# Nyström attention followed by a SiLU feed-forward layer on one core: four second-layer products, one landmark tree and some vector work are moved to other slots

## The chip, the cores and the metric

The kernel runs on one core of a Trainium2 chip. The metric is the device time of one execution in microseconds (us). Before the change three runs took 259.84, 260.09 and 260.16 us, with a median of 260.09 us. The engines are named as in the profile: PE is the matmul engine and PEld its weight loads, DVE the vector engine, ACT the scalar engine, POOL the GpSimd engine, SP the queue from which output writes and DMA transposes are issued.

## The reference

For each of 8 batches and 8 heads (576 tokens, 64 dimensions a head) the reference computes a Nyström approximation of attention and puts its result through a two-layer network:

```python
q_lm = q.reshape(B, H, 32, 18, D).mean(axis=3)      # 32 landmarks a head
k_lm = k.reshape(B, H, 32, 18, D).mean(axis=3)
A  = softmax(q    @ k_lm.T / sqrt(D))               # 576 x 32
Bm = softmax(q_lm @ k_lm.T / sqrt(D))               # 32 x 32
C  = softmax(q_lm @ k.T    / sqrt(D))               # 32 x 576
Z  = Bm.T / (norm1(Bm) * norminf(Bm) + 1e-6)
for _ in range(6):
    Z = 2 * Z - Z @ Bm @ Z
x = A @ Z @ C @ v                                   # 8 heads side by side: 4608 tokens x 512
h = x @ w_in                                        # 512 -> 2048
out = (h * sigmoid(h)) @ w_out                      # 2048 -> 512
```

## The kernel before

The work is a pipeline over batches, with the order of every engine written out by hand. Each engine executes its instructions in program order, and an instruction waits for semaphores of the engines and transfers whose data it needs.

**Periods and slots.** Batch b has a period of 16 slots. In slot s, `l1(s)` multiplies two 128-column blocks of the folded first layer (`mb`, which is Z·C·v·w_in of that batch) with the transposed attention matrix `AT` into a PSUM tile `hps`, and `act(s)` has ACT apply SiLU from `hps` into `gT`. Slots 0 to 7 cover the first half of the batch's tokens and 8 to 15 the second. `hps` comes from a ring of two PSUM tiles (`ps2`, two banks each), which is also used by the tiles `scp`, `sa`, `mpp`, `ctp` and, in some places, `lmp`. So a matmul into such a tile waits until the tile before last has been read.

**The second layer** is a queue. `l2_mm(n)` issues the next n products `ops` (`gT` block times `w_out`, 512 columns). After 16 products a block of 128 tokens is complete; ACT copies it to `ost`, and SP writes it out. The table `CNT` says how many products each slot of batches 0, 1 and 2 issues; later batches use `REST`. The products are the filler that PE does between steps that wait for other engines.

**The attention of the next batch** is computed inside the same slots. Its steps, each named by its method: scores and softmax of B and C (`b_scores`, `c_scores`, `c_max`, `c_exp`, `b_norm`, `b_expand`), the iteration for Z on PE and DVE (`f_mm`, `b_scale`, `f_out`, then pairs `ns_mm` on PE and `ns_step` on DVE, the last with `x_out`), C·v (`w_scale` takes reciprocals of C's sums on DVE in four small operations; `w_mm`, `w_out`), its product with Z (`z_mm`, `z_out`), and the fold with `w_in` (`m_unit` or `m_pair`: PE products, then copies into `mb` by DVE and ACT). The matrix A is normalized by `a_norm(i)`: a sum and a reciprocal on DVE and a multiplication on POOL (`an`). For batches 0 and 1, PE transposes A (`a_transpose`, copied by `a_out` into `AT`); from batch 2 on, DVE does (`a_back`). From batch 2 on, C's exponentials go to `eCT` by DMA transposes issued from SP, and A's scores go through DVE transposes `xs`, maxima `nm`, a subtraction on POOL (`a_sub`) and one exponential on ACT (`a_exp_all`).

**Landmarks.** Sums over 18 tokens are made by PE (`landmarks_pe`, tile `lmp`) or, from batch 2 on, by a tree of five additions on POOL (`landmarks_pool(b, j)`: tiles `lma`, `lmb`, `lmc`, `lmd`, `lmn`), each tree for two of the four loaded arrays `nat` of a batch (j = 0 or 2). `lm_t` transposes the landmarks on DVE.

**Loads** are issued from POOL's queue (`load_qk`, `load_v`), so each stands in line with POOL's arithmetic.

Batch 0's period has the attention of batch 1 from slot d = 2 on; in the code `r = s - d`. Batch 1's period has the attention of batch 2 from slot d = 3 on. In slot d of batch 1, `a_pair` computes the scores `sa` of batch 2 and `a_sub` follows on POOL. In slot d + 3 = 6, `f_mm` to the first `ns_mm` stand around the products. In slot 15 of batch 1, `lm_t` and `a_pair` of batch 3 are issued. The lines that matter before the change: `m_unit` at 735 to 756, `CNT` at 847, the landmark sum in slot 1 of batch 1 at 988 to 991, `rest` and `m_unit(2, ...)` at 1051 to 1061, the steps r = 5 to 8 at 1097 to 1120, and the trees at 1207.

Of the kernel before, what the change touches and what calls it, by code (L numbers as in the profile page):

```python
# [43 lines left out]
def kernel(  # L44
# [9 lines left out]
    nc = tc.nc  # L54
# [28 lines left out]
    def ps2(nm):  # L83
        return psh.tile([128, 2, 512], FP, tag="h", name=nm)
# [16 lines left out]
    def load_qk(b, js=(1, 0, 3, 2)):  # L101
        if b not in nat_t:
            nat_t[b] = loadp.tile([128, 4, SEG * Dh], BF, tag="nat", name="nat")
        nat = nat_t[b]
        for j in js:
            src = (q, k)[j % 2]
            g = j // 2
            nc.gpsimd.dma_start(
                out=nat[:, j, :],
                in_=src[b, 4 * g:4 * g + 4].rearrange("h (l t) d -> (h l) (t d)", t=SEG))  # L110
# [136 lines left out]
    class Att:  # L247
# [484 lines left out]
            copy(out=self.AT[:, :, self.ar[0]:self.ar[1]], in_=self.at)  # L732


        def m_unit(self, f, *copy, parts=1, between=None, pair=False, before=None):
            self.m_done = f + 1
            if f == 0:
                mb_t[self.b] = attp.tile([128, 2, DFF], BF, tag="mb", name="mb")
            if pair:
                m2 = ps2("mpp")  # L740
                m = [m2[:, 0, :], m2[:, 1, :]]
            else:
                m = [psa1("mp"), pso1("mp")]
            for j in range(4):
                for r in range(2):
                    p = slice(64 * r, 64 * r + 64)
                    mm(m[r][32 * j:32 * j + 32, :], self.zwT[p, j, :],
                       w_in_sb[p, j, 512 * f:512 * f + 512], start=True, stop=True)
            if before:
                before()  # L750
            for c0 in range(0, 512, 512 // parts):
                if c0 and between:
                    between()
                for r in range(2):
                    c = slice(c0, c0 + 512 // parts)
                    copy[1 if c0 else r](out=mb_t[self.b][:, r, 512 * f:512 * f + 512][:, c], in_=m[r][:, c])

# [80 lines left out]
    def l2_add(b, *blocks):  # L840
        for i in blocks:
# [2 lines left out]
            l2_state["queue"] += [(b, 128 * i, c, c + w) for c in range(0, DM, w)]  # L844


    CNT = {0: [0, 0, 0, 0, 4, 4, 2, 2, 4, 4, 3, 3, 2, 2, 1, 1],
           1: [1, 0, 1, 4, 2, 12, 12, 0] + [4] * 8,
           2: [8, 4, 12, 12, 3, 3, 2, 2, 3, 3, 3, 3, 3, 2, 2, 7]}
    REST = [3, 4, 12, 12, 3, 2, 2, 2, 4, 4, 4, 3, 3, 3, 3, 8]  # L850

# [20 lines left out]
    a = Att(0)  # L872
# [68 lines left out]
    for b in range(B):  # L941
# [3 lines left out]
        a0 = a  # L945
        a, ready = ready, None

        d = (2, 3)[b] if b < 2 else 0
# [5 lines left out]
        def act(s):  # L954
            l1_act(b, s, h.pop(s))

        for s in range(NDC):
# [3 lines left out]
            if s <= d and b == 0:  # L961
# [5 lines left out]
                elif s == 1:  # L967
                    a0.m_unit(1, nc.scalar.copy, nc.scalar.copy, parts=2,
                              between=lambda: act(1))
# [6 lines left out]
                if s == 0:  # L976
                    a = Att(1)
# [3 lines left out]
            elif not nxt or s <= d:  # L981
                l1(s)
                act(s)
                n = cnt[s]

                if s == 0 and b % 2:
                    l1_tail(b)
                if b == 1 and s == 1:
                    lp = ps2("lmp")[:, 0, :]
                    landmarks_pe(2, lp, 2, 2)  # L990
                    landmarks_out(2, lp, 2, 2)
# [44 lines left out]
            elif s == d + 2:  # L1036
# [11 lines left out]
                a.a_shift(0)  # L1048
                a.a_exp(0)

                def rest():
                    for i in (1, 2):
                        a.a_shift(i)
                        a.a_exp(i)
                    a.c_transpose(0)
                    a.b_expand()
                    l2_mm(2)
                    a.f_mm()
                    a.b_scale()

                a0.m_unit(2, nc.vector.tensor_copy, nc.scalar.copy, pair=True, before=rest)
                table(AF.Silu)
                a.f_out()
                a.c_out(0)
# [5 lines left out]
            elif b == 0:  # L1070
# [4 lines left out]
                if r == 3:  # L1075
                    load_qk(3, (1,))
                    act(s - 1)

                    def step():
                        a.ns_mm()  # L1080
                        a.ns_step()
                        l1(s)

                    a0.m_unit(3, nc.scalar.copy, nc.scalar.copy, before=step)
                    nc.vector.tensor_tensor(out=parity, in0=mask[:, 0:2, 0],
                                            in1=mask[:, 2:4, 0], op=OP.add)
                elif r == 4:
                    a.ns_mm()
                    a.ns_step()
                    act(s)  # L1090
                    a0.a_transpose(1)
                    a0.a_out(nc.vector.tensor_copy)
                    a.c_transpose(1)
                    a.c_out(1)
                    a.a_norm(0)
                    load_qk(3, (0,))
                elif r == 5:
                    act(s)
                    a.ns_mm()
                    a.ns_step()  # L1100
                    a.w_scale()
                    a.a_norm(1)
                elif r == 6:
                    a.ns_mm()
                    a.ns_step()
                    a.a_norm(2)
                    load_qk(3, (3,))
                elif r == 7:
                    a.ns_mm()
                    a.ns_step()  # L1110
                    load_qk(3, (2,))
                    landmarks_pool(2, 0)
                elif r == 8:
                    a.ns_mm(last=True)
                    a.x_out()
                    act(s)
                    l2_mm(n)
                    n = 0
                    a.a_transpose(0)
                    a.a_out(nc.vector.tensor_copy)  # L1120
                elif r == 9:
                    act(s)
                    transpose_qk(2, ORD[0])
                    l2_mm(n)
                    n = 0
                    a.w_mm()
                    a.w_out()
                elif r == 10:
                    a.z_mm()
                    a.z_out()  # L1130
                    transpose_qk(2, ORD[1])
                elif r == 12:
                    a.a_transpose(1)
                    a.a_out(nc.vector.tensor_copy)
                    transpose_qk(2, ORD[2])
# [60 lines left out]
            if b == 0:  # L1196
                if s == 3:
                    load_qk(2)
            elif b + 2 < B:

                if b == 1 and s == 9:
                    load_qk(4)
                if s == 14 and b + 4 < B:
                    load_qk(b + 4)
                if s == 7 + d // 2:
                    load_v(b + 2)
                if s in (4 + d, 8 + d):
                    landmarks_pool(b + 2, (s - 4 - d) // 2)

                if s == 13 and b > 1:  # L1210
                    ready = Att(b + 2)
                    ready.lm_t(0, 2)
                ts = (7, 8, 10, 12) if d == 0 else (8, 9, 10, 11)
                if s in ts:
                    transpose_qk(b + 2, ORD[ts.index(s)])
                if s == 15 and b == 1:
                    ready = Att(b + 2)
                    ready.lm_t(0, 2)
# [38 lines left out]
```

## Time and profile before

| | before |
|---|---|
| median of 3 runs | 260.09 us |
| the profiled execution's own time | 260.13 us |
| its span, first to last instruction | 258.4 us |
| PE busy | 243.5 us (94%) |
| ACT busy | 169.8 us (66%) |
| DVE busy | 163.4 us (63%) |
| POOL busy | 128.2 us (50%) |
| granted TensorE clock | 1.000 |

Rows of a timeline give the start in us from the span's start, the duration in us, the engine, the source line, the operation, what is written and read, and the shape; in brackets stands the engine's idle time before the instruction, and what ended it. Several similar instructions close together are merged into one row (x4), whose duration then goes from the first start to the last end. A row of the chain of waits gives start, share of the end's path in us, engine, tile and line. Matmuls overlap: the distance between two starts is shorter than one matmul's duration. Some matmul records are missing from the trace (554 of the products appear, against 592 loads of their weights), so a hole of about 0.22 us ahead of a product `ops` need not be a wait.

### The profile page before, as it was taken

What the parts mean: (1) busy time and instruction counts of PE and PEld (TensorE: products, weight loads), DVE (VectorE), ACT (ScalarE), POOL (GpSimd) and SP (SyncE); (2) the same over time, 40 slices, a digit from 0 to 9 for tenths busy, and PEclk for the clock granted to TensorE, in tenths of its full rate; (3) what the DMA queues carried; (4) which work ended last, traced back from release to release, by engine and by line L of the source; (5) the groups of instructions that cost most, each with busy time, mean ns of one, the idle gap of its engine ahead of it and who ended that gap; (6) DMA issues with size and microseconds to landing.
All of it is one profiled execution on the core that took longest, in us unless ns stands there. A gap on an engine that the chain in (4) does not pass through costs nothing.

```text
span 258.4 us, 6560 instructions
## 1 busy us (share of the span) xinstructions
PE 243.5 (94%) x2706; PEld 138.7 (54%) x2748; DVE 163.4 (63%) x375; ACT 169.8 (66%) x312; POOL 128.2 (50%) x156
## 2 busy tenths in 40 slices
PE   8979999989998999999999999999999999999994
PEld 2646555455554555556654564556545655556553
DVE  5878977858896859776885688667967545000000
ACT  2378975669746875778576957597669858445511
POOL 7716547713899379935993299319923030100000
PEclk9999999999999999999999999999999999999999
DMA  7999999971389993885289418122621500111122
GB/s 219 202 210 207 206 206 213 223 161 30 114 119 237 193 130 64 123 180 142 49 140 198 116 43 133 43 57 88 121 56 44 136 25 24 54 68 43 42 81 81
DMA packets 30061, 31.15 MB, mean 121 GB/s; under 512 B 10960, under 2 KB 21456, under 8 KB 30032
## 3 DMA queue, kind: packets, MB, share of 16 engines
q0 software_dynamic: 14816, 17.76, 42.0%
q1 hardware_dynamic: 15216, 12.98, 17.9%
q8 instruction: 21, 0.34, 0.5%
q14 instruction: 8, 0.07, 0.1%
HBM read 36.70 MB, written 9.44 MB: 179 GB/s over the span
## 4 chain that ended last, share of the span: by engine, by line
PE 73%; DVE 8%; POOL 7%; issue 4%; ACT 4%; DMA 3%; POOLq 0%; ACTq 0%
PE ops L80 39%; PE hps L80 20%; DMA eCT<-eC 3%; PE idle L80 3%; PE bb L80 2%; PE lmp L80 2%; POOL lma L232 2%; DVE cmx L449 2%; PE sa L80 2%; PE mp L80 2%; PE scp L80 1%; PE wp L80 1%; DVE nm L610 1%; PE mpp L80 1%; POOL xs L636 1%
## 5 line engine op out<-in xcount | busy, mean ns | idle before, releaser
L80 PE MATMUL ops<-w_out_sb,gT 128*128 128x512 bf16 (+1 forms) x554 | 138.6, 373 | 4.3 <-issue 3.6
L810 ACT ACTIVATE gT<-hps 128x576 bf16<-128x576 f32 (+2 forms) x128 | 82.6, 652 | 57.1 <-PE hps L80 54.9
L80 PE MATMUL hps<-AT,mb 128*128 128x288 bf16 (+2 forms) x512 | 83.0, 286 | 1.5 <-DVE xs L627 0.7
L80 PEld LDWEIGHTS <-gT 128*128 128x128 bf16 x592 | 54.2, 98 | 48.5 <-issue 8.8
L80 PEld LDWEIGHTS <-mb 128*128 128x128 bf16 x512 | 48.2, 98 | 27.4 <-issue 1.8
L203 DVE STREAM_TRANSPOSE qkT<-nat 128x576 f32<-128x576 f32 x32 | 39.1, 1243 | 0.2
L836 ACT COPY ost<-ops 128x512 f32<-128x512 f32 (+1 forms) x37 | 21.1, 572 | 14.6 <-PE ops L80 11.5
L232 POOL TENSOR_TENSOR lma<-nat 128x1152 f32<-128x1152 bf16 x11 | 26.2, 2381 | 0.4 <-DMA nat<-in_q_dram 0.3
L408 DVE SCALAR_TENSOR_TENSOR fx<-fx,bb 128x320 bf16<-128x320 bf16 (+1 forms) x39 | 17.9, 458 | 11.3 <-PE bb L80 10.5
L636 POOL TENSOR_TENSOR xs<-xs,nm 128x576 f32<-128x576 f32 x12 | 13.6, 1155 | 19.3 <-DVE nm L631 19.3
L776 DVE CAST mb<-mp 128x512 bf16<-128x512 f32 x28 | 18.0, 685 | 7.2 <-PE mp L80 7.2
L165 ACT ACT_TABLE_LOAD x16 | 20.5, 1283 | 1.1 <-PEq L1241 0.8
L1154 POOL COPY gate<-wsp 128x2 f32<-128x2 f32 x6 | 1.1, 186 | 30.7 <-DVE wsp L493 30.7
L692 POOL TENSOR_TENSOR an<-ex,arec 128x576 bf16<-128x576 bf16 x12 | 13.6, 1159 | 5.3 <-DVE arec L678 5.2
L80 PEld LDWEIGHTS <-fx 128*128 128x128 bf16 (+1 forms) x132 | 8.3, 94 | 12.2 <-DVE fx L408 5.2
L80 PE MATMUL bb<-fx 128*128 128x160 bf16 (+2 forms) x132 | 13.5, 212 | 1.2 <-DVE fx L408 1.1
L777 ACT CAST mb<-mpp 128x1024 bf16<-128x1024 f32 x14 | 14.2, 1012 | 0.0
L627 DVE STREAM_TRANSPOSE xs<-sa 128x576 f32<-128x576 f32 x12 | 8.7, 762 | 7.6 <-PE sa L80 7.6
L449 DVE TENSOR_REDUCE cmx<-scp 128x1 f32<-128x576 f32 x16 | 12.0, 752 | 0.5 <-PE scp L80 0.3
L663 DVE TENSOR_REDUCE arec<-ex 128x18 f32<-128x576 bf16 (+2 forms) x17 | 11.7, 689 | 0.0
L814 POOL COPY gT<-gT 128x1024 bf16<-128x1024 bf16 x4 | 4.1, 1037 | 14.9 <-ACT gT L810 14.9
L237 POOL TENSOR_TENSOR lmc<-lmb,lma 128x384 f32<-128x384 f32 x11 | 11.0, 1004 | 0.9
(120 smaller groups left out, 267.7 us busy)
## 6 DMA issues: line engine op xcount, KB each, us to landing
out_dram<-ost SPq DMA_DIRECT2D x35, 256.0 KB, 2.3
v<-in_v_dram POOLq DMA_DIRECT2D x8, 576.0 KB, 7.2
nat<-in_k_dram POOLq DMA_DIRECT2D x15, 288.0 KB, 7.8
nat<-in_q_dram POOLq DMA_DIRECT2D x15, 288.0 KB, 8.3
w_in_sb<-in_moe_w_in_dram POOLq DMA_DIRECT2D x4, 512.0 KB, 14.5
w_out_sb<-in_moe_w_out_dram POOLq DMA_DIRECT2D x4, 512.0 KB, 13.6
raw<-in_k_dram SPq DMA_DIRECT2D x1, 576.0 KB, 4.2
raw<-in_q_dram SPq DMA_DIRECT2D x1, 576.0 KB, 5.1
```

The costliest lines, as they stand in the source:

```text
L80: nc.tensor.matmul(out=o, lhsT=lhsT, rhs=rhs, start=start, stop=stop, skip_group_check=True)
L165: nc.scalar.activation(out=spare[:, 1:2], in_=spare[:, 0:1], func=func)
L203: nc.vector.transpose(out=o.rearrange("p (l t) -> p t l", t=SEG), in_=nat_t[b][:, j, :].bitcast(FP).rearrange("p (t l) -> p t l", l=L))
L232: nc.gpsimd.tensor_tensor(out=a1, in0=nat[:, :, 0:3 * w], in1=nat[:, :, 3 * w:6 * w], op=OP.add)
L408: nc.vector.scalar_tensor_tensor(out=n, in0=self.fx, scalar=2.0, in1=self.p, op0=OP.mult, op1=OP.add if self.tiled else OP.subtract)
L449: nc.vector.tensor_reduce(out=mx, in_=self.s[g][:, :, 0:HF], op=OP.max, axis=AX.XY, negate=True)
L636: nc.gpsimd.tensor_tensor(out=self.xs[:, i], in0=self.xs[:, i], in1=self.nm[:, i].unsqueeze(3).to_broadcast((128, 2, SEG // 2, L)), op=OP.add)
L692: nc.gpsimd.tensor_tensor(out=self.an[:, i].rearrange("p r t l -> p (r t) l"), in0=x, in1=r.unsqueeze(2).to_broadcast((128, SEG, L)), op=O ...
L776: nc.vector.tensor_copy(out=o[:, r, 0:512], in_=m[r])
L777: nc.scalar.copy(out=o[:, :, 512:1024], in_=m2)
L810: nc.scalar.activation(out=gT_t[b][:, 2 * s:2 * s + 2, o + c0:o + c1], in_=h[:, :, 0:c1 - c0], func=AF.Silu)
L836: nc.scalar.copy(out=ost[:, 0:hi - lo], in_=st["ps"][:, 0:hi - lo])
```

## The change

It has six parts.

1. `m_unit` gets a second callback. In slot 4 of batch 0 (r = 2), the shift and exponentials of A and the transposes of C stay ahead of the copies of `mb`; the expansion of B, two products, `f_mm` and `b_scale` come behind them. On PE nothing changes place; on DVE the copy into `mb` comes ahead of four small operations (`bdt`, `cs`, `n`, `nrm`) and no longer behind them.
2. The products of batch 0's slots 10 to 15 go from 3, 3, 2, 2, 1, 1 to 2, 2, 1, 1, 0, 2, four fewer. Those of batch 1's slots 0 to 6 go from 1, 0, 1, 4, 2, 12, 12 to 1, 1, 2, 7, 2, 12, 11, four more. The block of 16 that was finished in slot 15 of batch 0 is now finished in slot 2 of batch 1.
3. In slot 1 of batch 1 the product stands ahead of the landmark matmuls of batch 2.
4. `w_scale` of batch 1 moves from r = 5 to r = 8, behind `x_out`.
5. `a_norm(1)` of batch 1 moves from r = 5 to r = 6, and `a_norm(2)` from r = 6 to r = 7, each with its multiplication on POOL; the load of one array of batch 3 thereby comes ahead of the second multiplication.
6. Batch 3's tree for j = 0 moves from slot 7 to slot 0 of batch 1, and its tree for j = 2 from slot 11 to slot 7. On POOL the first now stands between the copy of `gT`'s tail and the subtractions of batch 2's `a_sub`; behind the second, the loads of batch 4 and those of batch 5 follow each other with no tree between.

```diff
-        def m_unit(self, f, *copy, parts=1, between=None, pair=False, before=None):
+        def m_unit(self, f, *copy, parts=1, between=None, pair=False, before=None,
+                   after=None):
...
+            if after:
+                after()
...
-    CNT = {0: [0, 0, 0, 0, 4, 4, 2, 2, 4, 4, 3, 3, 2, 2, 1, 1],
-           1: [1, 0, 1, 4, 2, 12, 12, 0] + [4] * 8,
+    CNT = {0: [0, 0, 0, 0, 4, 4, 2, 2, 4, 4, 2, 2, 1, 1, 0, 2],
+           1: [1, 1, 2, 7, 2, 12, 11, 0] + [4] * 8,
...
                 if b == 1 and s == 1:
+                    l2_mm(n)
+                    n = 0
                     lp = ps2("lmp")[:, 0, :]
...
-                def rest():
+                def first():
                     for i in (1, 2):
                         a.a_shift(i)
                         a.a_exp(i)
                     a.c_transpose(0)
+
+                def second():
                     a.b_expand()
                     l2_mm(2)
                     a.f_mm()
                     a.b_scale()
 
-                a0.m_unit(2, nc.vector.tensor_copy, nc.scalar.copy, pair=True, before=rest)
+                a0.m_unit(2, nc.vector.tensor_copy, nc.scalar.copy, pair=True, before=first,
+                          after=second)
...
                     a.ns_mm()
                     a.ns_step()
-                    a.w_scale()
-                    a.a_norm(1)
                 elif r == 6:
                     a.ns_mm()
                     a.ns_step()
-                    a.a_norm(2)
+                    a.a_norm(1)
                     load_qk(3, (3,))
                 elif r == 7:
                     a.ns_mm()
                     a.ns_step()
+                    a.a_norm(2)
                     load_qk(3, (2,))
                     landmarks_pool(2, 0)
                 elif r == 8:
                     a.ns_mm(last=True)
                     a.x_out()
+                    a.w_scale()
...
-                if s in (4 + d, 8 + d):
-                    landmarks_pool(b + 2, (s - 4 - d) // 2)
+                trees = (0, 7) if b == 1 else (4, 8)
+                if s in trees:
+                    landmarks_pool(b + 2, 2 * trees.index(s))
```

## The prediction

> **What bounds the kernel now.** I read the page first (spans, engines, chain), then the chain of waits over batches 0 and 1, then the timeline around every step that moves.
>
> ```profile
> PE 73%; DVE 8%; POOL 7%; issue 4%; ACT 4%; DMA 3%; POOLq 0%; ACTq 0%
> ```
>
> This is the chain that ended last: PE carries 73% of it, so what shortens the kernel is a wait of PE that goes away, or a product put where PE would have waited. After the wait at 96.43 us, quoted further down, the timeline shows none of PE's that is worth naming; whatever lead PE has there should reach the end. I therefore follow one number through the trace: by how much PE reaches each step earlier than before, the lead.
>
> **Slot 4 of batch 0: nothing.** Rows of the timeline:
>
> ```profile
> 32.30 0.59 ACT L756 CAST mb<-mpp 128x512 bf16<-128x512 f32 x1 [0.43 <-DVE mb L756]
> ```
> ```profile
> 35.00 1.62 POOL L697 TENSOR_TENSOR an<-ex,arec 128x512 bf16<-128x512 bf16 x2
> ```
> ```profile
> 36.67 0.44 PEld L725 LDWEIGHTS <-an 64*128 64x128 bf16 x4 [0.19 <-POOL an L697]
> ```
>
> ACT's copy waited 0.43 us for DVE's. With DVE's copy ahead of the four small operations, ACT's comes some 0.4 us earlier, and the first layer's matmuls behind it. But PE then transposes batch 0's second part of A, whose multiplication on POOL ends at 36.62; it hangs on a load issue and DVE sums that don't move. PE already waited for it. The lead there goes back to 0.
>
> **The sums and the scaling: 0.55 us.** DVE, then PE:
>
> ```profile
> 39.42 0.15 DVE L487 RECIPROCAL wsc<-csum 128x1 f32<-128x1 f32 x1
> 39.59 0.33 DVE L489 RECIPROCAL wsc<-csum 64x1 f32<-64x1 f32 x2
> 39.95 0.43 DVE L493 TENSOR_TENSOR wsp<-wsc,parity 128x4 f32<-128x4 f32 x1
> ```
> ```profile
> 41.18 0.43 DVE L408 SCALAR_TENSOR_TENSOR fx<-fx,bb 128x320 bf16<-128x320 bf16 x1
> ```
>
> ```profile
> 40.57 0.71 PE L80 MATMUL hps<-AT,mb 128*128 128x320 bf16 x4
> 41.66 0.31 PE L80 MATMUL bb<-fx 128*128 128x160 bf16 x2 [0.39 <-DVE fx L408]
> 41.81 1.03 PE L80 MATMUL ops<-w_out_sb,gT 128*128 128x512 bf16 x4
> 42.68 0.71 PE L80 MATMUL hps<-AT,mb 128*128 128x320 bf16 x4
> 43.22 0.20 PE L80 MATMUL bb<-fx 128*128 128x32 bf16 x2
> ```
>
> Two prices come from here: a product takes PE (42.68 - 41.81)/4 = 0.217 us, a slot's first layer 43.22 - 42.68 = 0.54. Without a wait, `bb` at 41.66 would start at 40.57 + 0.54 = 41.11. It waits because `ns_step` stands behind w_scale and a_norm(1) on DVE. After the change nothing stands between: lead 0.55. The a_norms fall into the next two slots, where DVE has room: the first took from `wsp`'s end at 40.38 to 41.18, 0.8 us, and a slot lasts 42.68 - 40.57 = 2.1. Their multiplications on POOL are needed only by the transposes of slots 10 and 14; that a load of batch 3 is now issued ahead of the second costs POOL's queue nothing that PE waits for.
>
> **Slot 10: DVE becomes the bound.** Here two products are taken out (0.43), but w_scale now stands in front of a_out:
>
> ```profile
> 43.46 0.45 DVE L424 SCALAR_TENSOR_TENSOR xb<-fx,bb 64x64 bf16<-64x64 bf16 x2 [0.96 <-PE bb L80]
> 44.45 0.56 DVE L732 COPY AT<-atp 128x768 bf16<-128x768 bf16 x1 [0.54 <-PE atp L725]
> ```
> ```profile
> 46.17 0.42 DVE L512 TENSOR_TENSOR wz<-wp,wsp 128x256 bf16<-128x256 f32 x1
> ```
>
> `xb` starts at 43.46 - 0.55 = 42.91 and ends at 43.36. w_scale takes 0.53 us up to `wsp`, and `wsp` itself 0.43 as above or less:
>
> ```profile
> 65.27 0.16 DVE L493 TENSOR_TENSOR wsp<-wsc,parity 128x4 f32<-128x4 f32 x1
> ```
> ```profile
> 39.32 1.04 POOL L697 TENSOR_TENSOR an<-ex,arec 128x512 bf16<-128x512 bf16 x1 [2.04 <-ACT gT L810]
> ```
>
> The long `wsp` ended at 40.38, just after POOL's multiplication (40.36); the short one, in batch 1, ran with POOL idle. Moved, `wsp` comes about 0.1 us behind POOL's last multiplication by my order, so I take 0.16. That puts the copy of `AT` at 43.36 + 0.69 = 44.05, or 0.1 sooner as neighbours on an engine overlap a little (the pair at 81.59 and 81.99 below: 0.05; for three pairs an estimate). `wz` follows the copy's start by 46.17 - 44.45 = 1.72, near 45.67: lead 0.5 for `wz` and the `z_mm` that waits for it. With 0.43 for `wsp` it is 0.25. PE itself would be nearly 1 us early; the two products buy nothing here.
>
> The Trainium skill ("SBUF — State Buffer", section "SBUF: two separate sides") says that a VectorE operation with two SBUF inputs and a GpSimd operation that reads SBUF exclude each other for a whole instruction. The pair of ends 40.36 and 40.38 agrees. By that rule any overlap would hold `wsp` to the end of POOL's instruction, and the kernel would come to about 258.55 and not 258.3.
>
> **Slots 12 to 15 and the start of batch 1.** Three products less and one more: 3 x 0.217 gives a lead of 1.15 before the last, of which I take off 0.1, an estimate between nothing and one product, because `hps` in slot 14 now comes close to ACT's previous `gT`. So 1.05 when ACT takes slot 15's `gT`, 0.83 when PE starts batch 1. There the chain of waits runs over ACT:
>
> ```profile
> 50.88 0.70 ACT gT L810
> 51.58 0.90 ACT mb L777
> 52.49 0.49 ACT ost L836
> 52.98 0.56 ACT gT L810
> 53.54 0.04 issue
> 53.58 1.17 PE lmp L80 x18
> ```
>
> The block's end moves to slot 2, so `ost` (0.49) leaves this chain, and `lmp` is released at 53.58 - 1.05 - 0.49 = 52.04. PE needs longer: its second first-layer group waits for the copy `mb` that ended at 51.58 + 0.90 = 52.48 and now ends at 51.43, then its four matmuls of 288 columns (0.54 x 288/320 = 0.49) and the added product: about 52.2. I take a lead of 1.3. Slot 2's added product lowers it to 1.1. `ost` now stands between two `gT` copies, with one slot's room. Its write goes out on SP some 2 us later, still ahead of batch 2's transposes; nothing else moves on that queue. Slot 3 gets three more products, in front of this wait:
>
> ```profile
> 57.88 0.28 PE L80 MATMUL hps<-AT,mb 128*128 128x288 bf16 x1 [0.66 <-DVE xs L627]
> ```
>
> They take 0.65; of the 0.66 idle, some is the pipeline's own, and I take 0.5. Lead behind them 0.95. `xs`, with its lead of 1.1, is then ready 0.15 before PE asks for it; that is the cover.
>
> **The tree in slot 0: must fit.** It stands on POOL behind the tail copy; `a_sub` and the gate copy queue behind it, and ACT's exponential waits for `a_sub`.
>
> ```profile
> L108 POOL DMA_DIRECT2D nat<-in_q_dram x1: 594/594/594, 40.3 to 40.3; - x1
> ```
> ```profile
> DMA to landing us min/median/max: 13.5/13.5/13.5
> ```
> ```profile
> 59.20 2.27 POOL L636 TENSOR_TENSOR xs<-xs,nm 128x576 f32<-128x576 f32 x2 [6.52 <-DVE nm L631]
> ```
> ```profile
> 62.91 1.15 ACT L643 ACTIVATE ex<-xs 128x1152 bf16<-128x1152 f32 x1
> ```
> ```profile
> 76.42 2.41 POOL L232 TENSOR_TENSOR lma<-nat 128x1152 f32<-128x1152 bf16 x1
> ```
> ```profile
> 81.59 0.45 POOL L240 TENSOR_TENSOR lmn<-lmd,lmc 128x128 bf16<-128x128 f32 x1
> 81.99 0.58 POOL L108 DMA_DIRECT2D nat<-in_k_dram  x1
> ```
>
> Its array of batch 3 was issued at 40.3 and landed at 53.8. A tree takes 82.04 - 76.42 = 5.62, so it ends near 59.45, although POOL was idle for 6.52 us before. `a_sub` (2.27) then runs 59.5 to 61.8; the exponential can start at 61.85, or 1.06 earlier than before. My lead is 0.95: the cover is 0.1 us, and beyond it every 0.1 of delay costs 0.1, because ACT's chain releases the next first layer in slot 7.
>
> Slot 6's removed product shortens the way to `ns_mm`; DVE's later `ns_step`s come earlier and with them a wait of PE's weight load:
>
> ```profile
> 72.43 0.11 PEld L80 LDWEIGHTS <-fx 128*128 128x128 bf16 x2 [0.51 <-DVE fx L408]
> ```
>
> Worth 0.2, one product: lead 1.15.
>
> **The tree that leaves slot 11: 0.4, and the transposes behind it: 0.25.**
>
> ```profile
> 82.45 0.32 PE L80 MATMUL sa<-qkT,lmc 32*32 32x288 bf16 x8 [0.36 <-DVE lmc L274]
> ```
> ```profile
> L466 SPq DMA_TRANSPOSE eCT<-eC x2: 1217/1254/1290, 88.3 to 89.7; - x2
> ```
> ```profile
> DMA to landing us min/median/max: 6.7/7.1/7.4
> ```
> ```profile
> 96.43 0.24 PEld L80 LDWEIGHTS <-eCT 96*32 96x32 bf16 x24 [0.25 <-DMA eCT<-eC]
> ```
>
> The late tree ended at 82.04, `lm_t` followed, and `sa` waited 0.36. The tree would have held any lead there; with both trees early, `sa` follows the products: lead 1.55. The four loads of batch 5, behind that tree at 81.99, are issued some 6 us earlier, so that most of them should have landed when `eCT`'s transposes start on the DMA engines, at 88.3 less the lead. If they took as long as before, the second would land near 89.7 - 1.55 + 6.7 = 94.85 and PE need it at 96.43 - 0.25 - 1.55 = 94.63, the same wait; so this is worth 0 to 0.25, and I take 0.25, since the loads are what the transposes shared the engines with: lead 1.8.
>
> **Sum.** 0.5 (slot 10), 0.83 (slot 0), 1.3, 1.1, 0.95 (slot 4), 1.15, 1.55, 1.8. The profiled execution's own time is 260.13, 0.04 above the median, so the difference between them doesn't matter: 260.13 - 1.8 = **258.3 us**.
>
> **The rivals.** *Batch 0's lead is lost on DVE* (w_scale and the copy push `wz` back to 46.17). For it: DVE would have 2.8 us of work between `xb`'s new start and `wz` with next to no gap; against it: the durations above leave 0.25 even with the long `wsp`. Then the leads are 0 at slot 10, 0.33, 0.8, 0.6, 0.45, 0.65, 1.05, 1.3: 258.8. Chance 0.18.
>
> *The lead is spent at `eCT`.* If the transposes still land at 96.4, because DMA bandwidth and not the issue sets them, PE waits there whatever it gained: 260.1. For it: landings of 6.7 to 7.4; against it: the earlier loads. Chance 0.09.
>
> *Slower: the tree in slot 0 comes too late.* These rows are the load issued ahead of the one above:
>
> ```profile
> L108 POOL DMA_DIRECT2D nat<-in_k_dram x1: 607/607/607, 36.7 to 36.7; - x1
> ```
> ```profile
> DMA to landing us min/median/max: 15.7/15.7/15.7
> ```
>
> If the later one took as long, it would land at 56.0, the tree end at 61.7, `a_sub` at 64.0, and the exponential start 1.15 later than before. The gains of 0.4 and 0.25 still come: 0.5 slower, 260.6. It decides for slower from a landing at about 55.5, that is 1.7 us later than shown. Against it: the load's issue isn't moved. Chance 0.08.
>
> **Numbers.** My forecast has 0.65. What a measurement can tell from no change is 0.2% (0.5 us). Faster: 0.65 + 0.18 = 0.83; same 0.09; slower 0.08. The range takes in the first two cases: below, 258.0, where the cover of 0.1 is used up and the ACT estimate costs nothing; above 259.4, where also half of the second case's gain is lost.
>
> **What would show it.** In the changed profile: `bb` in slot 9 follows the first layer at once; `wz` near 45.7; `lmp` near 52.3 with `ost` behind it; no wait before `hps` at 56.9; `lma` starts near 53.8, and `ex` isn't released by POOL; `sa` of batch 3 near 80.9 without a wait for `lmc`; `eCT` landing in well under 6.7. I am wrong if `ex` waits for `a_sub`, if `wz` stays at 46.2, or if PE waits for `eCT`.

## The result, and the profile after

The changed kernel took 258.41 us (median of 4 runs, 257.98 to 258.98), the kernel before in the same comparison 260.12 us (4 runs, 259.84 to 260.26). The ratio is 0.9935, with a 95% interval of 0.9917 to 0.9953. The forecast was 258.3 us. The profiled execution of the changed kernel is the longest of its four, 258.98 us, so the two traces differ by 258.98 - 260.13 = -1.15 us and not by the 1.7 us of the medians. That difference between profile and median is worth explaining first.

The page after, its chain that ended last:

```profile
PE 84%; DMA 7%; DVE 3%; ACT 1%; issue 1%; POOL 1%; SPq 0%; POOLq 0%; ACTq 0%
PE ops L80 49%; PE hps L80 23%; DMA w_out_sb<-in_moe_w_out_dram 5%; PE bb L80 3%; DMA raw<-in_q_dram 2%; PE mp L80 2%; PE scp L80 2%; PE sa L80 1%; PE lmp L80 1%; PE mpp L80 1%; PE wp L80 1%; POOL an L697 1%; DVE cmx L449 1%; DVE qkT L203 0%; PE atp L725 0%
```

The 2.65 us over ACT's `gT`, `mb` and `ost` into batch 1 (50.88 to 53.54 before), about 1% of the span, no longer stand in the chain. ACT's whole share fell from 4% to 1%; the rest of that fall is in other stretches. DMA rose from 3% to 7%, and the name behind it is new: the load of `w_out`, which nobody changed. The timeline shows how it enters. First POOL before the change (the last row, PE's, is for the table below):

```profile
31.30 0.53 POOL L108 DMA_DIRECT2D nat<-in_q_dram  x1 [2.10 <-DMA w_out_sb<-in_moe_w_out_dram]
34.13 0.80 POOL L114 DMA_DIRECT2D v<-in_v_dram  x1 [2.30 <-PE bb L80]
...
97.17 0.30 PE L80 MATMUL bb<-fx 128*128 128x160 bf16 x2
```

And the same stretch after, on POOL, ACT, PE and PEld:

```profile
32.25 0.53 POOL L108 DMA_DIRECT2D nat<-in_q_dram  x1 [1.50 <-DMA w_out_sb<-in_moe_w_out_dram]
35.09 0.80 POOL L114 DMA_DIRECT2D v<-in_v_dram  x1 [2.31 <-DVE arec L663]
35.95 1.61 POOL L697 TENSOR_TENSOR an<-ex,arec 128x512 bf16<-128x512 bf16 x2
...
31.47 0.57 ACT L757 CAST mb<-mpp 128x512 bf16<-128x512 f32 x1
...
32.01 0.60 PE L80 MATMUL ops<-w_out_sb,gT 128*128 128x512 bf16 x2 [0.65 <-DMA w_out_sb<-in_moe_w_out_dram]
...
37.04 0.11 PEld L725 LDWEIGHTS <-an 128*128 128x128 bf16 x2 [1.10 <-POOL an L697]
37.62 0.44 PEld L725 LDWEIGHTS <-an 64*128 64x128 bf16 x4 [0.46 <-POOL an L697]
```

ACT's copy of `mb` came 0.83 us earlier than before (32.30 to 31.47), and PE spent it twice: waiting 0.65 us for `w_out` and then for `an`. In this execution `w_out` landed 0.95 us later (the issue of `nat` that waits for it went from 31.30 to 32.25), the load of v for batch 2 was issued 0.96 later, and `an`, queued behind that load on POOL, started 0.95 later (35.00 to 35.95). The row of v names PE's `bb` in one trace and DVE's `arec` in the other, so the name alone doesn't settle what it waited for. In the trace the second of `w_out`'s four transfers ends at 33.55 before and at 34.51 after, and v's issue begins 0.58 us later in both: I read this as a wait for that transfer, one of those ahead of it in POOL's queue. The lateness starts ahead of `w_out`: the issue of `nat` that waits for the load of `w_in` already stands at 30.21 and not at 28.67.

So at slot 4 the profiled execution was 0.95 us behind the one before. Everything later in batch 0 starts from there. The steps of the prediction, with the start in both traces:

| step | before | after | lead | lead counted from the landing (+0.95) | forecast |
|---|---|---|---|---|---|
| `bb` of slot 9 | 41.66 | 42.06 | -0.40 | 0.55 | 0.55 |
| `wz` | 46.17 | 46.62 | -0.45 | 0.50 | 0.5 |
| `gT` of slot 15 | 50.88 | 50.74 | 0.14 | 1.09 | 1.05 |
| `lmp` | 53.58 | 53.11 | 0.47 | 1.42 | 1.3 |
| `hps` of slot 4, batch 1 | 57.88 | 57.79 | 0.09 | 1.04 | 0.95 |
| PE's weight load `fx` behind slot 6 | 72.43 | 72.05 | 0.38 | 1.33 | 1.15 |
| `sa` of batch 3 | 82.45 | 81.63 | 0.82 | 1.77 | 1.55 |
| `bb` behind the first `wp` from `eCT` of batch 3 | 97.17 | 96.06 | 1.11 | 2.06 | 1.8 |

Every increment has the forecast size within 0.1 us. What the forecast lacked is the term of 0.95, which isn't of the change. Taken by the letter, one of the prediction's signs of being wrong is met here, since `wz` stands behind 46.2; only with the landing taken out does it have its lead. Rows of the timeline after for these steps, on DVE, PE, ACT and PEld, and then the transposes `eCT`:

```profile
44.86 0.16 DVE L493 TENSOR_TENSOR wsp<-wsc,parity 128x4 f32<-128x4 f32 x1
46.62 0.41 DVE L512 TENSOR_TENSOR wz<-wp,wsp 128x256 bf16<-128x256 f32 x1
...
42.06 0.30 PE L80 MATMUL bb<-fx 128*128 128x160 bf16 x2
53.11 1.17 PE L80 MATMUL lmp<-nat,ident 128*128 128x128 bf16 x18
57.79 0.65 PE L80 MATMUL hps<-AT,mb 128*128 128x288 bf16 x4
81.63 0.70 PE L80 MATMUL sa<-qkT,lmc 32*32 32x288 bf16 x32
96.06 0.30 PE L80 MATMUL bb<-fx 128*128 128x160 bf16 x2
...
50.74 0.70 ACT L813 ACTIVATE gT<-hps 128x640 bf16<-128x640 f32 x1 [0.41 <-PE hps L80]
...
72.05 0.11 PEld L80 LDWEIGHTS <-fx 128*128 128x128 bf16 x2 [0.50 <-DVE fx L408]
95.13 0.45 PEld L80 LDWEIGHTS <-eCT 96*32 96x32 bf16 x48 [0.24 <-issue]
```
```profile
L466 SPq DMA_TRANSPOSE eCT<-eC x2: 1227/1228/1228, 87.5 to 88.9; - x2
...
DMA to landing us min/median/max: 5.6/6.0/6.4
```

`lmp`, `hps` and `sa` have no bracket: ACT no longer releases `lmp`, and the waits of 0.66 for `xs` and 0.36 for `lmc` are gone. The weights `eCT` load in one go of 48, where two halves had waited 0.24 and 0.25; the transposes landed after 5.6 to 6.4 us and not 6.7 to 7.4.

The tree in slot 0, the step on which the forecast had a cover of only 0.1 us (POOL, DVE, ACT of after):

```profile
54.66 2.37 POOL L232 TENSOR_TENSOR lma<-nat 128x1152 f32<-128x1152 bf16 x1 [2.12 <-DMA nat<-in_q_dram]
60.22 2.27 POOL L636 TENSOR_TENSOR xs<-xs,nm 128x576 f32<-128x576 f32 x2
...
59.69 0.17 DVE L307 TENSOR_SCALAR bbs<-bmx 128x2 f32<-128x2 f32 x1
61.73 0.83 DVE L328 TENSOR_TENSOR bm<-pb,brec 128x64 bf16<-128x64 f32 x1
...
62.41 0.21 ACT L459 ACTIVATION_READ_ACCUMULATOR eC<-scp,cbs 128x1 f32 x1
62.52 1.16 ACT L643 ACTIVATE ex<-xs 128x1152 bf16<-128x1152 f32 x1
```

Its array landed at 54.53 and not 53.8 (the load's issue had moved with `an`, from 40.3 to 41.3), `a_sub` ended at 62.49, and `ex` started at 62.52. ACT's own chain would have released it at 62.50 (0.09 behind the accumulator read, as in the kernel before, 62.82 to 62.91). Here both came together, so the cover was just used up.

### The profile page after: what moved, and what is told of

Its sections match the earlier page's. It is cut to its first block, busy times and chain, and to the rows that moved or that the text cites. A ratio compares the mean times of both kernels' runs of the same rounds, so it can differ in the third digit from the quotient of the medians.

```text
span 257.2 us, 6602 instructions
## 1 busy us (share of the span) xinstructions
PE 248.2 (96%) x2748; PEld 138.9 (54%) x2748; DVE 163.7 (64%) x375; ACT 169.5 (66%) x312; POOL 128.2 (50%) x156
## 4 chain that ended last, share of the span: by engine, by line
PE 84%; DMA 7%; DVE 3%; ACT 1%; issue 1%; POOL 1%; SPq 0%; POOLq 0%; ACTq 0%
PE ops L80 49%; PE hps L80 23%; DMA w_out_sb<-in_moe_w_out_dram 5%; PE bb L80 3%; DMA raw<-in_q_dram 2%; PE mp L80 2%; PE scp L80 2%; PE sa L80 1%; PE lmp L80 1%; PE mpp L80 1%; PE wp L80 1%; POOL an L697 1%; DVE cmx L449 1%; DVE qkT L203 0%; PE atp L725 0%
## 5 line engine op out<-in xcount | busy, mean ns | idle before, releaser
L80 PE MATMUL ops<-w_out_sb,gT 128*128 128x512 bf16 (+1 forms) x592 | 146.7, 374 | 0.7 <-DMA w_out_sb<-in_moe_w_out_dram 0.7
L80 PEld LDWEIGHTS <-fx 128*128 128x128 bf16 (+1 forms) x132 | 8.4, 94 | 11.5 <-DVE fx L408 4.7
L80 PE MATMUL bb<-fx 128*128 128x160 bf16 (+2 forms) x132 | 13.5, 212 | 0.5 <-DVE fx L408 0.3
L235 POOL TENSOR_TENSOR lmb<-lma 128x384 f32<-128x384 f32 x11 | 11.0, 998 | 0.9
```

The costliest lines, as they stand in the source:

```text
L80: nc.tensor.matmul(out=o, lhsT=lhsT, rhs=rhs, start=start, stop=stop, skip_group_check=True)
```

## The experiments

Each ran in five rounds beside the kernel before, whose medians there were 260.09 to 260.29 us. The theory under test is called the lead theory: the terms of the prediction add up, less what the transfers of the first 35 us hold. Its rivals stand with each run.

**The changed kernel again.** No edit.

> The changed kernel once more, timed beside the others. In its first profile the load of w_out landed 0.95 us later than in the profile before the change, and the rest of batch 0 stood 0.95 late with it. Lead theory (each part of the change gives PE a lead that reaches the end, late loads aside): about 258.2 us where w_out lands as it did before the change, about 259 where it lands 0.95 late, so a spread of 1 us that goes with the landing. Rival (the leads of batches 0 and 1 are lost on the way, and only the tree that leaves slot 11 pays): always about 259.4.

258.30 us (258.00 to 258.68, 6 runs), ratio 0.9922 (0.9907 to 0.9938). Its profiled execution is of 258.4 us. Two executions of one kernel can now be compared; the timeline of this one, on POOL, ACT, DVE and PE:

```profile
31.65 0.53 POOL L108 DMA_DIRECT2D nat<-in_q_dram  x1 [1.95 <-DMA w_out_sb<-in_moe_w_out_dram]
35.35 1.62 POOL L697 TENSOR_TENSOR an<-ex,arec 128x512 bf16<-128x512 bf16 x2
...
61.84 0.19 ACT L459 ACTIVATION_READ_ACCUMULATOR eC<-scp,cbs 128x1 f32 x1
62.17 1.16 ACT L643 ACTIVATE ex<-xs 128x1152 bf16<-128x1152 f32 x1
...
61.20 1.01 DVE L328 TENSOR_TENSOR bm<-pb,brec 128x64 bf16<-128x64 f32 x1
...
65.91 0.65 PE L80 MATMUL hps<-AT,mb 128*128 128x288 bf16 x4 [0.29 <-ACT gT L813]
```

`w_out` came 0.60 us earlier than in the first profile (32.25 to 31.65), `an` 0.60, and the whole execution took 0.58 less (258.98 to 258.40). In this pair the landing passes straight into the time: from `an` to the end they took 223.03 and 223.05 us (258.98 - 35.95, 258.40 - 35.35). The leads of the table come out again, too: counted from `an` (0.35 behind the kernel before), `bb` of slot 9 at 41.47, `wz` at 46.02, `lmp` at 52.50 and `sa` at 81.05 give 0.54, 0.50, 1.43 and 1.75. (`bm`, the row of DVE, is taken up further down.) And with batch 0 earlier, the cap shows: `ex` started 0.33 after the accumulator read in front of it where 0.09 is usual, 0.24 late, held by `a_sub`, and PE waited 0.29 for the `gT` behind it. That is one of the prediction's "I am wrong if". Yet it cost no time: at `sa` of batch 3 this execution is ahead of the first by 0.58 again (81.63 to 81.05).

**Both trees back in slots 7 and 11.**

```diff
-                trees = (0, 7) if b == 1 else (4, 8)
-                if s in trees:
-                    landmarks_pool(b + 2, 2 * trees.index(s))
+                if s in (4 + d, 8 + d):
+                    landmarks_pool(b + 2, (s - 4 - d) // 2)
```

> The changed kernel with batch 3's trees back in slots 7 and 11. Lead theory: the waits of batch 3's scores (0.36) and of eCT (0.25) come back and the lead of about 1 us at slot 7 stays, so 259.1 us. Landing theory (a_sub behind the tree in slot 0 caps the lead, at about 1 us when the load lands at 53.8 and at about 0.4 when it lands 0.6 later): without the tree the cap is gone, and it loses less, 258.8. Rival (only the tree pays): 260.1, as before the change.

259.08 us (258.81 to 259.53, 6 runs), ratio 0.9950 (0.9934 to 0.9965). The two waits are back, `sa` for the late tree and PE's weight loads for `eCT` (PE and PEld of the timeline, then the transposes' time from issue to landing):

```profile
81.67 0.70 PE L80 MATMUL sa<-qkT,lmc 32*32 32x288 bf16 x32 [0.57 <-DVE lmc L274]
...
95.30 0.24 PEld L80 LDWEIGHTS <-eCT 96*32 96x32 bf16 x24 [0.36 <-DMA eCT<-eC]
95.83 0.24 PEld L80 LDWEIGHTS <-eCT 96*32 96x32 bf16 x24 [0.30 <-DMA eCT<-eC]
```
```profile
DMA to landing us min/median/max: 6.9/7.3/7.7
```

The trees' move is worth 259.08 - 258.30 = 0.8 us by the medians, and these two waits are where it shows (forecast: 0.4, and 0.25 at `eCT`). That a late tree lengthens the transposes isn't shown by this run alone; a later one, with the load of v moved, speaks against it.

**The sums and the scaling back at r = 5 and 6.**

```diff
                 elif r == 5:
...
+                    a.w_scale()
+                    a.a_norm(1)
                 elif r == 6:
...
-                    a.a_norm(1)
+                    a.a_norm(2)
                     load_qk(3, (3,))
                 elif r == 7:
...
-                    a.a_norm(2)
                     load_qk(3, (2,))
...
                     a.x_out()
-                    a.w_scale()
```

> The changed kernel with w_scale and the a_norms of batch 1 back in r = 5 and 6. Lead theory: the matmul bb of slot 9 waits 0.4 to 0.55 us again; but DVE then has less to do in slot 10, so the lead at z_mm falls from 0.5 to about 0.2: 258.7 us. Landing theory: the exponential of batch 2 is set by the tree in slot 0 and not by the lead, so nothing changes: 258.4.

258.59 us (258.07 to 258.80, 6 runs), ratio 0.9930 (0.9914 to 0.9946). The interval overlaps that of the changed kernel, so the median difference of 0.3 isn't established. The traces say more: from `an` to the end this execution took 258.07 - 34.78 = 223.29 us, and the two of the changed kernel 223.03 and 223.05, so this part is worth some 0.24. In its profile `an` starts 0.22 ahead of before (34.78) and `wz` 0.47 (45.70); so, counted from `an`, 0.25 of `wz`'s 0.5 remains without this part. The two products that leave slot 10 fit it: the copy of `AT` now waits 0.32 for PE's transposes where it waited 0.54.

**The products back in their old slots.**

```diff
-    CNT = {0: [0, 0, 0, 0, 4, 4, 2, 2, 4, 4, 2, 2, 1, 1, 0, 2],
-           1: [1, 1, 2, 7, 2, 12, 11, 0] + [4] * 8,
+    CNT = {0: [0, 0, 0, 0, 4, 4, 2, 2, 4, 4, 3, 3, 2, 2, 1, 1],
+           1: [1, 0, 1, 4, 2, 12, 12, 0] + [4] * 8,
```

> The changed kernel with the old counts of products in batches 0 and 1. Lead theory: the lead stays at 0.5 from slot 10 to slot 4 of batch 1 (the copy ost stands in front of batch 1's first gT again, and the waits before lmp and hps of slot 4 are unfilled), then 0.36 and 0.25 come on top: 258.9 to 259.0 us. Landing theory: the tree sets the exponential, and the products buy nothing: 258.4.

259.78 us (258.83 to 260.31, 12 runs), ratio 0.9980 (0.9968 to 0.9992). I missed this one by 0.8 us: almost the whole gain goes. DVE, POOL and ACT of this kernel say why:

```profile
60.25 1.01 DVE L307 TENSOR_SCALAR bbs<-bmx 128x2 f32<-128x2 f32 x1
...
60.07 2.27 POOL L636 TENSOR_TENSOR xs<-xs,nm 128x576 f32<-128x576 f32 x2
...
63.78 1.15 ACT L643 ACTIVATE ex<-xs 128x1152 bf16<-128x1152 f32 x1
```

`bbs`, two columns wide, took 1.01 us where it took 0.17 in the changed kernel. It ended at 61.26, and the first of `a_sub`'s two instructions, which started at 60.07 and took 1.16, at 61.23. So DVE stood still while POOL's instruction ran, and the maxima, the exponentials and `ex` came late behind it. In the changed kernel the earlier lead lets `bbs` pass before `a_sub` starts (59.86 against 60.22), and it is `bm` that meets it: 0.83 for `bm`, which ends at 62.56 just behind `a_sub` at 62.49, against 0.23 in the kernel before.

The Trainium skill ("SBUF — State Buffer", section "SBUF: two separate sides") has this: a VectorE operation in a two-port mode, or one with two SBUF inputs against a GpSimd operation that reads SBUF, and the GpSimd operation exclude each other for the whole instruction. By `bm` (two SBUF inputs, 0.23 to 0.83) the trace agrees. `bbs` reads one tensor, and no run shows in which mode it ran; that it was held is measured. The prediction weighed the rule at `wsp` only, where no multiplication of POOL ran in the end, and overlooked it where the tree pushes `a_sub`.

**The first tree in slot 3, behind `a_sub`.** If the tree's place ahead of `a_sub` does harm, it could stand behind.

```diff
-                trees = (0, 7) if b == 1 else (4, 8)
+                trees = (3, 7) if b == 1 else (4, 8)
```

> The changed kernel with batch 3's first tree behind a_sub, in slot 3 of batch 1, in place of ahead of it in slot 0. Landing theory alone (what costs is that a_sub waits for the tree, which waits for the load): a_sub runs as soon as its maxima are there, 258.2 us. Exclusion theory (a DVE operation with two SBUF inputs waits for the POOL instruction that is running): the tree's first addition (2.4) and second (1.0) then run where DVE computes bm and bdt, bm takes about 1.5 us instead of 0.23, f_mm on PE comes about 1 us later, 259.2 us.

259.37 us (258.84 to 260.40, 12 runs), ratio 0.9971 (0.9959 to 0.9984): a microsecond worse. Now the tree's additions run against the small operations on DVE (DVE, POOL, PE):

```profile
60.92 1.69 DVE L328 TENSOR_TENSOR bm<-pb,brec 128x64 bf16<-128x64 f32 x1
62.92 0.82 DVE L319 TENSOR_TENSOR bdt<-bme,mask 128x256 bf16<-128x256 bf16 x1
...
60.16 2.36 POOL L232 TENSOR_TENSOR lma<-nat 128x1152 f32<-128x1152 bf16 x1
62.60 0.99 POOL L235 TENSOR_TENSOR lmb<-lma 128x384 f32<-128x384 f32 x1
...
63.80 0.29 PE L80 MATMUL bb<-bdt 128*128 128x128 bf16 x2 [0.83 <-DVE bdt L319]
```

`bm` ended at 62.61, with `lma` (62.52), and `bdt` at 63.74, behind `lmb` (63.59); PE waited 0.83 us for `bdt`. The exclusion was to give 259.2, the landing alone 258.2: the exclusion decides.

**Without the second callback.** `second()` runs behind `first()`, ahead of the copies of `mb`, as in the kernel before.

```diff
-                a0.m_unit(2, nc.vector.tensor_copy, nc.scalar.copy, pair=True, before=first,
-                          after=second)
+                def rest():
+                    first()
+                    second()
+
+                a0.m_unit(2, nc.vector.tensor_copy, nc.scalar.copy, pair=True, before=rest)
```

> The changed kernel without the second callback of m_unit: DVE's copy into mb behind bdt, cs, n and nrm again. As predicted (the 0.4 us are lost at the transposes that wait for POOL's an): no difference, 258.3 us. If the 0.4 us reach the end: 258.7.

258.35 us (257.92 to 258.61, 5 runs), ratio 0.9924 (0.9908 to 0.9941): no difference from the changed kernel. This confirms "slot 4: nothing", and its reason: PE's weight load still waits 0.46 us for `an` at the end of the slot.

**The load of v moved behind `a_norm(0)`, from slot 4 to slot 6.** If `an` hangs on the landing of `w_out` only through the load in front of it on POOL, the load can go elsewhere.

```diff
                 a.f_out()
                 a.c_out(0)
-                load_v(2)
                 a0.a_norm(1)
...
                     a.a_norm(0)
                     load_qk(3, (0,))
+                    load_v(2)
```

> The changed kernel with the load of batch 2's v issued later: not ahead of batch 0's an in slot 4 but behind batch 3's first two arrays in slot 6. Landing theory: an no longer waits for a landing of w_out, so it ends near 36.2 and the transposes behind it come 0.4 to 0.8 us earlier; batch 3's first two arrays land 1.5 to 2.9 us earlier, so the tree in slot 0 ends ahead of batch 2's maxima and caps nothing: 257.6 us. Lead theory without landings: the order of loads changes nothing on PE, 258.3.

257.50 us (257.45 to 257.63, 5 runs), ratio 0.9894 (0.9877 to 0.9911): faster than both kernels, and the runs lie within 0.18 us of each other, where those of the changed kernel spread over 0.68. POOL, PE, DVE and ACT:

```profile
31.33 0.53 POOL L108 DMA_DIRECT2D nat<-in_q_dram  x1 [2.23 <-DMA w_out_sb<-in_moe_w_out_dram]
34.51 1.62 POOL L697 TENSOR_TENSOR an<-ex,arec 128x512 bf16<-128x512 bf16 x2 [2.65 <-ACT gT L813]
51.77 2.37 POOL L232 TENSOR_TENSOR lma<-nat 128x1152 f32<-128x1152 bf16 x1 [0.62 <-DMA nat<-in_q_dram]
57.55 2.27 POOL L636 TENSOR_TENSOR xs<-xs,nm 128x576 f32<-128x576 f32 x2 [0.18 <-DVE nm L631]
...
60.54 0.23 DVE L328 TENSOR_TENSOR bm<-pb,brec 128x64 bf16<-128x64 f32 x1
...
61.26 1.15 ACT L643 ACTIVATE ex<-xs 128x1152 bf16<-128x1152 f32 x1
```

Two holds went at once. `an` starts with `w_out` at its old time yet 0.49 us ahead of before. And the tree's array, now ahead of v in the queue (v at 40.41), is issued at 39.82 and lands 11.5 us later, not 13.5, so that `lma` starts at 51.77 and not at 54.66: the tree ends before `nm`, `a_sub` waits for DVE and no longer for the tree, `bm` is back at 0.23, and `ex` starts 1.65 us earlier than before the change. For the time, however, the traces show only the first hold: from `wz` to the end this execution took 257.62 - 45.23 = 212.39 us, and the two of the changed kernel 212.36 and 212.38. The whole gain is there at `wz` (46.02 to 45.23); that the tree ends earlier adds nothing behind it.

**The same without the second callback.**

> Both: the load of v later, and m_unit without its second callback. With an no longer held by a landing, the callback's 0.4 us should no longer be lost: 258.0 us, 0.4 above the kernel with the late load alone. If the callback is worth nothing for another reason: the same as that kernel.

257.96 us (257.80 to 258.04, 5 runs), ratio 0.9911 (0.9895 to 0.9926). The callback, worth nothing above, is worth 0.46 us here by the medians, and the runs of the two kernels don't overlap. As expected, ACT's gain passes on once `an` isn't held. The two profiled executions, one of the slower of the kernel with the callback and the fastest without it, show less of it: 0.26 at ACT's copy and 0.17 at `bb` of slot 9 (40.68 against 40.85). How the rest arises isn't shown.

**The load of v moved, the products in their old slots.**

> The changed kernel with the load of v moved to slot 6, and the second-layer products in their old slots. Exclusion theory: without the moved products the changed kernel lost 1.5 us, of which some 0.6 was DVE's two-column operation bbs held behind the subtraction a_sub, which the tree had made late. With the load moved the tree ends some 2 us sooner, a_sub stands where it stood before the change, and bbs is held 0.45 at most: only the lead of the block's copy and of the products is lost, 0.8 to 1.0: 258.4. Rival 'the products alone are worth 1.5': 259.0.

258.32 us (258.16 to 258.52, 6 runs), ratio 0.9931 (0.9918 to 0.9943). `a_sub` starts at 58.15 here and `bbs` still meets its first instruction, but near its end: it takes 0.43, not 1.01, and the products are worth 258.32 - 257.50 = 0.8 us, not 1.5. The rest of the loss above fits the collision.

**The load of v moved, the trees in slots 7 and 11.**

> The changed kernel with the load of v moved to slot 6, and both trees in their old slots 7 and 11. Lead theory: lost are the wait of sa for the late tree (0.4 plus the lead that it holds) and the wait for eCT (0.3): 258.3 to 258.5. Rival 'the tree in slot 0 costs something by its place even when its array is early': less is lost, 258.0.

258.23 us (258.09 to 258.39, 6 runs), ratio 0.9926 (0.9914 to 0.9939). The trees' move is worth 0.7 us here, 0.8 above: so by the medians an early array adds nothing that can be told apart to what the tree's move is worth, as long as the lead is there. But only one of the two expected waits is back (PE and PEld):

```profile
80.84 0.70 PE L80 MATMUL sa<-qkT,lmc 32*32 32x288 bf16 x32 [0.56 <-DVE lmc L274]
...
94.33 0.45 PEld L80 LDWEIGHTS <-eCT 96*32 96x32 bf16 x48 [0.24 <-issue]
```

The loads of batch 5 stand behind the late tree again, and yet the transposes land after 5.7 to 6.5 us. What all fourteen traces show is that the second transpose lands 3.8 to 3.9 us behind the last of these loads: before the change at 96.4 behind 92.6, after it at 94.5 behind 90.7, here at 93.8 behind 89.9. In the changed kernel that load is issued 5.8 us earlier than before (83.60 to 77.84) but takes 12.8 us to land and not 9.0, so it lands 1.9 earlier. Why it lands early here too, issued at 82.07, is open.

**The kernel before, with only the load of v moved.**

> The kernel before with one line moved: the load of v for batch 2 goes from slot 4 of batch 0, ahead of A's second and third multiplication, to slot 6, behind a load of batch 3. Theory 'two covers': in the changed kernel this move was worth 0.8 us because it freed two things, A's multiplication in slot 4 (0.4) and the array that the tree in slot 0 waits for (the cap on the exponential, 0.4). The kernel before has neither the callback nor that tree, so only what PE waited for the multiplication (0.2 to 0.3) is left: 259.9 to 260.1. Rival 'the load itself': the load's place is worth the same in any kernel of this form: 259.5.

259.69 us (259.46 to 260.46, 12 runs), ratio 0.9986 (0.9976 to 0.9995), 0.1 to 0.6 us by the interval. This lies between my two theories. 0.8 is excluded, so part of the load's worth in the changed kernel comes through the change; but it is more than the 0.2 to 0.3 I expected from PE's wait for `an`. In its trace `bb` of slot 9 starts 0.35 ahead of before. Two medians above resolve it: the kernel before has no second callback, and in the changed kernel without it the load's move is worth 258.35 - 257.96 = 0.39 us, about the 0.40 of here; with the callback it is 0.80. So by the medians about half of the 0.8 is the load itself, in either kernel, and the other half comes with the callback.

**The load of v moved, `w_scale` one step earlier.** It stands behind the `ns_step` of r = 7, where DVE had a gap of 0.41 us ahead of `xb`.

```diff
                     a.ns_step()
+                    a.w_scale()
                     a.a_norm(2)
...
                     a.x_out()
-                    a.w_scale()
```

> The changed kernel with the load of v moved to slot 6, and C's scaling (w_scale) one step earlier, behind the seventh Newton step and not behind x_out. Lead theory: DVE is the bound of slot 10 (PE waited 0.23 for wz in the kernel with the load moved); it has a gap of 0.4 there ahead of xb, and wz comes earlier by 0.2 to 0.4, of which PE can use 0.23: 257.3. Rival 'wsp is held by POOL's multiplication again': no gain, 257.5, or up to 0.3 slower.

257.38 us (257.31 to 257.60, 5 runs), ratio 0.9895 (0.9880 to 0.9911). The ranges overlap, so this isn't shown to beat 257.50. In the profile the step does what it should and pays the exclusion again:

```profile
41.92 0.40 DVE L493 TENSOR_TENSOR wsp<-wsc,parity 128x4 f32<-128x4 f32 x1
44.93 0.41 DVE L512 TENSOR_TENSOR wz<-wp,wsp 128x256 bf16<-128x256 f32 x1
...
41.24 1.06 POOL L697 TENSOR_TENSOR an<-ex,arec 128x512 bf16<-128x512 bf16 x1
```

`wsp` has 0.40 and ends with POOL's `an` (42.30 and 42.32), not 0.16; `wz` still comes 0.30 earlier than at 45.23.

## Why the prediction was right, and where it was off

*Slot 4, nothing:* right, shown by leaving the callback out (258.35 against 258.30). But the reason given (that `an` "hangs on a load issue and DVE sums that don't move") took the load's issue as a fixed time. It goes with the landing of `w_out`, which differed by 0.95 us between the two profiles and by 0.60 between two executions of the changed kernel. That is the term that was left out. Without the load in that place the same edit is worth 0.46.

*The sums and w_scale, 0.55, and slot 10, 0.5:* right in the trace, 0.55 and 0.50 from the landing. So the rival that batch 0's lead is lost on DVE fell. `wsp` took 0.16 as chosen; it started at 44.86, and POOL's last multiplication had ended at 44.62. The rival with 0.43, and the rule by which the kernel would come to 258.55, weren't called on there. How much of the 0.5 this part gives by itself isn't settled by the times, since leaving it out gave overlapping intervals; counted from `an`, the traces give it 0.24, and the other 0.25 stayed when it was left out.

*Slots 12 to 15 and ACT's chain, 1.05 and 1.3:* measured 1.09 and 1.42, and `lmp` is no longer released by ACT.

*The tree in slot 0:* the arithmetic of the tree (5.6 us, then 2.27) was right and its start was off: 54.66 and not 53.8, because I let the landing stay where it was although its issue follows `an`. The slower rival named this place; its size was small. `a_sub` ended 0.7 later than forecast. That held `ex` back by 0.24 in the second profile, but it cost the kernel nothing that shows: "every 0.1 of delay costs 0.1" didn't hold for this 0.24, since from `wz` to the end both profiles took the same as the kernel whose tree was early (212.36, 212.38 and 212.39). What the prediction missed at this place is the other half of the mechanism: `a_sub` late doesn't only hold ACT, it holds DVE's `bbs` or `bm`. With the products left out, that goes with a loss of 0.7 us more (1.5 against 0.8).

*Slot 6, 0.2, `sa`, 0.4, and `eCT`, 0.25:* measured as increments of the lead 0.29, 0.44 and 0.29. At `eCT` the size was right and the reason only half right. The loads are what the transposes go with, but the forecast had most of them landed when the transposes start, and the last one landed at 90.7, behind the issue of both transposes (87.5 and 88.9). It landed 1.9 us earlier than before, and so did the second transpose. So the rival that the lead is spent at `eCT` was nearer to the mechanism; it fell because PE was only 0.8 us earlier by then. That the 0.25 was met is in part luck.

*The sum:* 1.8 forecast, 2.06 from the landing less 0.95 in the first profile; the medians differ by 1.7 and 2.0 us. The number came out because the leads were sized right and the profile of before was close to its median. That last point is luck: in one comparison the kernel before ran from 259.67 to 260.90 us, so a forecast from another of its executions could have been off by half a microsecond with the same steps.

Why the landing varies isn't settled: up to there the two programs are the same, and the runs show only that it does, and that `w_in` is late with `w_out`.

## What to carry to other kernels

An operation that stands on a queue behind a load's issue has that load's wait as its own, and the engine that the profile names need not be what it waited for: compare the same row in two executions, and if its start moves with a transfer's landing, move the load and not the operation. When work is pushed later on POOL, list which small DVE operations it will now run beside, since each can be held until POOL's instruction ends; a tree placed ahead or behind decided here between 258.3 and 259.4. A part that is worth nothing may only be covered: the callback went from 0 to 0.46 us when the wait behind it was taken away. And an operation that ends late need not cost anything: `ex` came 0.24 late, and the end stayed where it was.

## What the runs showed of the hardware that was not expected

- The landing of the same load, with the same program up to it, lay 0.6 us apart in two executions of one kernel, and that difference passed into the time (0.58). With the load of v moved, five executions of the changed kernel lay within 0.18 us; those of the kernel before, with the same move, still spread over 1.0 us (259.46 to 260.46, 12 runs).
- A DVE operation of 128 x 2 elements took 1.01 us beside a POOL subtraction that had just started, 0.43 beside one near its end, and 0.17 without; one of 128 x 64 with two inputs took 0.22 to 0.23 alone and 0.83, 1.01 and 1.69 beside POOL.
- One load put behind another in the queue shortened the other's way from issue to landing from 13.5 to 11.5 us.
- The second DMA transpose of batch 3 landed 3.8 to 3.9 us behind the last load issued ahead of it, in fourteen traces, whether that load was issued 4.7 us ahead of the first transpose (before) or 9.7 (after).
